# Sparse attention with soft mixture of experts on one core: the first transfers in a fixed order, larger load pieces, another table of priorities

## The chip, the core and the metric

The kernel runs on one NeuronCore of a Trainium2 chip. All data are fp32. The core has a matrix engine (TensorE, PE in the profile), VectorE (DVE), ScalarE (ACT), GpSimd (POOL) and SyncE (SP), which only issues transfers here. Each takes its instructions from its own list in the order in which they were written; semaphores hold an instruction back until what it needs is there. Transfers run on 16 DMA engines that all issuers share. The metric is the time of one execution on the device in microseconds (us), as the median of several runs.

## What is computed

Block-sparse attention feeds a soft mixture of experts. Cut to what matters:

```python
# q, k, v: [4, 8, 768, 64]; 24 blocks of 32 rows; 3 sampled blocks per block row
scores = (q @ k.T) / 8
mask   = |bi - bj| <= 1, or bi or bj is the first or the last block, or bj in sampled_blocks[bi]
attn   = softmax(where(mask, scores, -1e9)) @ v          # -> x [3072, 512]

logits = x @ phi                                          # [3072, 32]: 8 experts x 4 slots
d = softmax over the 3072 rows;  slots = d.T @ x          # [32, 512]
slot_out[e] = relu(slots[e] @ w1[e]) @ w2[e]              # FF = 1024
out = softmax over the 32 slots of logits @ slot_out      # [3072, 512]
```

## The kernel before

**Attention.** The four batches follow one another. The first and the last block row of a batch see all 24 blocks ("dense", two tasks per batch); the other 22 are taken in eleven pairs ("pair"). These tasks are numbered n = 0, 1, 2 ... over all batches; batch 0 begins with a dense task (n = 0), then the first pair (n = 1). For a pair, POOL and ACT copy the key blocks that it sees into a staging buffer `kst` (window and global blocks on POOL at L538 and L540, the three sampled blocks on ACT at L546 or on POOL at L548), and POOL copies the sampled value blocks into `vrs` (L564). Its queries are loaded (`q`, L407, 128 KB) and scaled in place by POOL (L583) or ACT (L581). PE makes scores `s` (L619), DVE their negative maximum `nm` (L636), ACT the exponentials `p` (L641), DVE transposes them in blocks of 32 into `ptt` (L648), and PE multiplies them with the values `v` and `vrs` (`av`, L713). DVE divides and writes the tile `x` (L706 to L708). The dense tasks do the same with `sd`, `nb`, `pd`, `ptd`, `avd` (L815, L841, L846, L850), directly from `ktile` and `v`. Score tiles `s`, `sd` and the warm-up's `st` take turns in four PSUM buffers.

**Grouping.** Four finished tiles `x` make a group: PE transposes them (`mxt`, L906), makes logits (`ml`), and adds up the dispatched rows with a running maximum (`md`, `ms`).

**Experts.** Afterwards 64 weight pieces of 512 KB are multiplied in turn: `w1` (`pf`, L1331), then `w2` (`pso`, L1339); the combine (`po`, L1435) follows in two column halves, and SP stores the result, 6.29 MB.

**Places of the weights.** 11 pieces have room from the beginning. 15 more are loaded into the room of attention's `ktile`, `v0`, `ptd` and again `ktile` (there they are called `kw`) towards the end of attention; these are the early weights. The late weights are issued after the planned part: ten into free room (`w26` to `w31`, `w36` to `w39`), six into the room of `v1`, and two into the last two `ptt` buffers (`w42`, `w43`); each further piece follows when an earlier one has been used. All are issued on SP.

**What sets the order.** In attention and grouping each step is a task of a plan (`Plan.add`): a function, the engines that may run it with a cost, the tasks that it depends on, a key, the buffers that it takes (`acq`) and the bytes of its transfer. A list scheduler goes through these tasks: of those that can start soonest it takes the one with the smallest key plus `BEHIND[kind]`, where the kind is the function that made the task. So a table of 79 numbers sets the order of PE, DVE, ACT, POOL and SP, and the choice of engine where there are several. `after` is a dependence on another task's start alone. What is written outside the plan ahead of it (in the kernel before: `ident`, an identity matrix built by POOL, and `sel4`, built from it by DVE and ACT) stands where it is written. Behind the plan PE, DVE, ACT and POOL keep the order of the code, and SP's is set by the framework's scheduler.

**The start.** POOL fills `ident` (masks.py:197 and 199). DVE and POOL clear the halves of `v0`, ACT those of `v1` (L465, by scaling a column of `ident` with 0). ACT loads the sampled block numbers (`scr`, L357) and the `q` of n = 1. SP loads the first `q`, K of batch 0 in four pieces (L420), `phi` (L1118), V of batch 0 in eight pieces (L431), and further `q`. PE runs 12 matmuls on `ident` to warm up (L479).

**Pieces.** `LR = 32` is the number of rows in one K load of the batches 1 to 3 and in one load of an early weight; `VC` the number of value blocks in one V load (13 for batch 0, 7 for the others); `LCOLS` cuts the last `kw` and the first ten late weights into two loads of 512 columns.

Of the kernel before, what the change touches and what calls it, by code (L numbers as in the profile page):

```python
# [15 lines left out]
ALU = mybir.AluOpType  # L16
# [27 lines left out]
LR, RATE = 32, 0.22  # L44

LC = 512
# [13 lines left out]
LCOLS = [slice(c, c + LC) for c in range(0, WP, LC)]  # L60
# [6 lines left out]
BEHIND = {0: -83.25, 1: -13.2, 2: -52.5, 3: 75.2, 4: 62.8, 5: 11, 6: -77.2, 7: -48.45, 8: -12.95, 9: -4.65, 10: 6.3,  # L67
# [30 lines left out]
FETCH, PACKET = 3.5, 256  # L98
# [10 lines left out]
class Plan:  # L109
# [29 lines left out]
    def plan(self, turn, best=1e9):  # L139
# [14 lines left out]
        while avail:  # L154
# [50 lines left out]
            elif e == "SP":  # L205
                dma = max(dma, st + 2.2) + self.byte[t] / 0.39e6
                fin = dma + 0.3
            elif e == "NONE":
                fin = st
            else:  # L210
                fin = en + LAG[e]
# [69 lines left out]
def attn_moe_kernel(ctx, tc, qT, kT, vtab, sampled, phi, w1, w2, out):  # L281
# [49 lines left out]
    def w_of(n, c):  # L331
# [5 lines left out]
    make_identity(nc, ident)  # L337
    sel4 = const.tile([P, P], F32, name="sel4")
    DVE.tensor_reduce(out=sel4[:, 0:NS], in_=ident.rearrange("p (c s) -> p s c", c=4),
                      axis=AX.X, op=ALU.add)  # L340
    for c in range(1, 4):
        ACT.copy(out=sel4[:, c * NS:(c + 1) * NS], in_=sel4[:, 0:NS])
# [68 lines left out]
    VC = lambda b: 7 if b else 13  # L411
# [48 lines left out]
    t_idx = add(lambda t: index_load(), ("ACT", 2.0), [], -40)  # L460

    def clear(b, a):
        half = vbuf[b][:, a * VH:(a + 1) * VH]
        if b:
# [3 lines left out]
    t_zero = [[add(clear(b, a), (("DVE", "POOL")[a], 2.7) if b == 0 else ("ACT", 2.85), [], -45 if b == 0 else -35 + a)  # L468
               for a in range(2)] for b in range(2)]

# [1057 lines left out]
```

## Time and profile before

| | |
|---|---|
| median of 3 runs | 310.47 us (310.13, 311.16, 310.47) |
| profiled execution | 312.11 us, of which span 310.3 us from the first instruction to the last |
| mean granted PE clock | 0.969 |
| instructions | 17664 |
| ACT, POOL busy | 175.4 us (57%), 179.6 us (58%) |
| DMA | 60.30 MB, mean 194 GB/s; HBM read 52.86 MB, written 6.29 MB |
| instruction loads (queue q8) | 57 packets, 0.93 MB |

All durations below come from the one profiled execution. Its time outside the span is 312.11 − 310.3 = 1.8 us. A row of the timeline has start, duration, engine, line, operation, tile written and tiles read, count, and in brackets the idle time of the engine ahead of it and what ended that. "ACTq" and "SPq" are the instruction queues of ACT and SP; their rows are the issues of transfers. A releaser is inferred from semaphores: with several, it is the last by the profile.

### The profile page before, as it was taken

How to read it: one execution, taken by the hardware profiler on the slowest of the kernel's cores; microseconds unless marked ns; L12 is line 12 of the kernel's file. 1: busy time of each engine (PE TensorE's matmuls, PEld its weight loads, DVE VectorE, ACT ScalarE, POOL GpSimd, SP SyncE). 2: the span in 40 equal slices, each digit the busy share in tenths (PEclk: the TensorE clock that was granted, in tenths of full speed). 3: DMA queues.
4: the chain of work that ended last, by engine and by line, in shares of the span. 5: the costliest groups of instructions: out<-in, count | busy, mean ns of one | idle time of the engine just before them, and what ended most of it. 6: DMA issues, size and time to landing. Idle time of an engine off the chain costs nothing.

```text
span 310.3 us, 17664 instructions
## 1 busy us (share of the span) xinstructions
PE 277.2 (89%) x7181; PEld 198.6 (64%) x7181; DVE 217.1 (70%) x500; ACT 175.4 (57%) x525; POOL 179.6 (58%) x491
## 2 busy tenths in 40 slices
PE   4388998999999799999999999999997899999950
PEld 4137876676777567768676777877676673355540
DVE  7477996768989487998998878998876225012350
ACT  6657786763677586647877863697630141102440
POOL 5589479964946968784589967569766014000000
PEclk9979999999999979999999999999997999999996
DMA  7924556320256743024465420677689999999998
GB/s 239 228 60 124 167 168 181 111 88 3 60 171 183 209 118 109 5 89 139 137 201 158 127 72 23 204 214 220 191 222 311 380 359 413 406 410 406 323 270 273
DMA packets 31971, 60.30 MB, mean 194 GB/s; under 512 B 5265, under 2 KB 18706, under 8 KB 31890
## 3 DMA queue, kind: packets, MB, share of 16 engines
q1 hardware_dynamic: 31744, 59.04, 59.7%
q8 instruction: 57, 0.93, 1.3%
q14 instruction: 24, 0.20, 0.2%
q10 hardware_dynamic: 146, 0.13, 0.2%
HBM read 52.86 MB, written 6.29 MB: 191 GB/s over the span
## 4 chain that ended last, share of the span: by engine, by line
PE 75%; DVE 9%; issue 4%; ACT 2%; DMA 2%; POOL 2%; POOLq 1%; SPq 1%; ACTq 0%; DVEq 0%
PE av L713 32%; PE s L619 11%; PE avd L713 5%; PE pso L1339 5%; PE pf L1331 5%; PE mxt L906 4%; PE sd L815 3%; DMA ktile<-in_kT_dram 2%; PE ms L991 2%; DVE ptd L850 2%; PE st L479 2%; PE po L1435 2%; PE ml L941 2%; DVE x L708 2%; DVE nm L636 1%
## 5 line engine op out<-in xcount | busy, mean ns | idle before, releaser
L564 POOL COPY vrs<-v 128x260 f32 x264 | 95.8, 405 | 30.8 <-PE av L713 23.0
L641 ACT ACTIVATE p<-s,nm 128x256 f32<-128x256 f32 x176 | 73.5, 475 | 15.8 <-DVE nm L636 12.1
L713 PE MATMUL av<-v,ptt 64*64 64x130 f32 (+2 forms) x1728 | 76.8, 290 | 1.2 <-PE md L982 0.8
L713 PEld LDWEIGHTS av<-v,ptt 64*64 64x64 f32 (+2 forms) x1728 | 51.2, 134 | 26.8 <-issue 19.4
L636 DVE TENSOR_REDUCE nm<-s 128x2 f32<-128x512 f32 x88 | 55.1, 680 | 5.6 <-PE s L619 5.2
L619 PE MATMUL s<-kst,q 64*32 64x256 f32 x1408 | 50.3, 386 | 8.3 <-POOL q L583 4.9
L648 DVE STREAM_TRANSPOSE ptt<-p 128x512 f32<-128x512 f32 x88 | 56.2, 682 | 1.7 <-ACT p L641 1.5
L540 POOL COPY kst<-ktile 128x384 f32<-128x384 f32 x88 | 42.9, 507 | 14.2 <-PE s L619 13.2
L713 PE MATMUL av<-vrs,ptt 64*32 64x130 f32 x2112 | 46.5, 278 | 3.5 <-issue 3.5
L546 ACT ACTIVATE kst<-ktile 128x128 f32 x186 | 41.5, 302 | 11.6 <-PE s L619 8.5
L619 PEld LDWEIGHTS s<-kst,q 64*32 64x32 f32 x1408 | 31.2, 107 | 17.3 <-POOL q L583 5.6
L713 PEld LDWEIGHTS av<-vrs,ptt 64*32 64x32 f32 x2112 | 35.9, 106 | 5.4 <-issue 5.3
L448 ACT COPY xT<-mxt 128x512 f32<-128x512 f32 (+1 forms) x22 | 12.5, 566 | 27.0 <-PE mxt L906 25.9
L713 PE MATMUL avd<-v,ptd 64*64 64x130 f32 x768 | 23.2, 271 | 1.3 <-DVE ptd L850 1.2
L713 PEld LDWEIGHTS avd<-v,ptd 64*64 64x64 f32 x768 | 21.8, 132 | 3.3 <-PE s L619 2.2
L548 POOL COPY kst<-ktile 128x128 f32 x78 | 19.9, 293 | 0.2 <-issue 0.2
L846 ACT ACTIVATE pd<-sd,nb 128x384 f32<-128x384 f32 x32 | 16.9, 579 | 4.3 <-DVE nb L841 4.1
L581 ACT ACTIVATE q<-q 128x256 f32<-128x256 f32 x27 | 11.2, 417 | 13.2 <-DMA q<-in_qT_dram 13.1
L815 PE MATMUL sd<-ktile,q 64*32 64x384 f32 x256 | 17.1, 504 | 1.3 <-ACT p L641 1.3
L706 DVE TENSOR_SCALAR rs<-av 128x8 f32<-128x8 f32 (+1 forms) x27 | 4.2, 157 | 19.7 <-PE av L713 19.5
L906 PEld LDWEIGHTS mxt<-ident,x 128*128 128x128 f32 x96 | 10.9, 147 | 11.2 <-DVE nm L636 2.5
L906 PE MATMUL mxt<-ident,x 128*128 128x128 f32 x96 | 16.9, 298 | 1.2 <-DVE x L695 0.9
(122 smaller groups left out, 305.2 us busy)
## 6 DMA issues: line engine op xcount, KB each, us to landing
w<-in_w_dram SPq DMA_DIRECT2D x17, 512.0 KB, 9.7
q<-in_qT_dram SPq DMA_DIRECT2D x47, 128.0 KB, 2.5
w<-in_w_dram SPq DMA_DIRECT2D x44, 128.0 KB, 3.3
out_dram<-ob SPq DMA_DIRECT2D x22, 256.0 KB, 3.2
ktile<-in_kT_dram SPq DMA_DIRECT2D x48, 96.0 KB, 2.7
v<-in_w_dram SPq DMA_DIRECT2D x8, 512.0 KB, 10.2
v<-in_vtab_dram SPq DMA_DIRECT2D x36, 113.8 KB, 3.2
v<-in_w_dram SPq DMA_DIRECT2D x24, 128.0 KB, 3.6
```

The lines of the kernel that those rows point to most:

```text
L540: POOL.tensor_copy(out=st[:, :, w:w + 96], in_=kv[:, :, (i - 1) * BLK:(i + 2) * BLK])
L546: ACT.activation(out=st[:, :, o:o + BLK], in_=src, func=AF.Copy, scale=1.0)
L548: POOL.tensor_copy(out=st[:, :, o:o + BLK], in_=src)
L564: POOL.tensor_copy(out=st[:, :, j:j + 1, :], in_=vf[:, :, ds(t.vals[j], 1), :])
L619: PE.matmul(u.s[r][32 * p:32 * p + 32, j, :], lhsT=u.q[s_, p, j, :], rhs=kd[j][0][s_, p, :], start=True, stop=True)
L636: DVE.tensor_reduce(out=u.nm[r], in_=u.s[r], axis=AX.X, op=ALU.max, negate=True)
L641: ACT.activation(out=u.p[r][:, j, :], in_=u.s[r][:, j, :], func=AF.Exp, bias=u.nm[r][:, j:j + 1], scale=1.0)
L648: DVE.transpose(out=T.pt[r][:, :, 2 * w:2 * w + 2, :].rearrange("p k j q -> p j k q"), in_=u.p[r].rearrange("p j (k q) -> p j k q", k=8))
L713: PE.matmul(av[:, r * 2 * D1:(r + 1) * 2 * D1].rearrange("p (a d) -> p a d", a=2), lhsT=lhsT, rhs=rhs, start=start, stop=stop)
L815: PE.matmul(u.s[r][k][32 * p:32 * p + 32, :], lhsT=T.dq.q[s_, p, j, :], rhs=kt[s_, p, 384 * k:384 * (k + 1)], start=True, stop=True)
L846: ACT.activation(out=u.p[r][k], in_=u.s[r][k], func=AF.Exp, bias=u.nb[r], scale=1.0)
L906: PE.transpose(T.px[:, c, :], T.x[:, c * P:(c + 1) * P], ident)
```

## The change

Five things are changed.

1. `make_identity` and the making of `sel4` become tasks of the plan (`t_ident`, `sel_head`, `sel_rest`); what reads `ident` or `sel4` depends on them.
2. The first transfers are chained by `after` in a fixed order (`seq`): the first `q`, K, the `q` of n = 3 and n = 4, V in an interleaved order, `phi`. ACT issues the `q` of n = 1 right behind the index load, and clears `v1` only behind that.
3. `LR` becomes 64 and `VC` 13 for all batches: K, V and the early weights are loaded in pieces about twice as large.
4. `LCOLS` goes: the last `kw` and the first ten late weights are loaded whole.
5. `BEHIND` gets other numbers (82 kinds now), and four of the planner's costs change: `FETCH`, SP's bytes per us, and ACT's cost of an issue.

SP's first rows, before (with the number of the tile behind each name):

```order
L407 DMA q0_97<-in_qT_dram 128x256
L420 DMA ktile_112<-in_kT_dram 128x2x384 x4
L1118 DMA phis_80<-in_phi_dram 128x128
L431 DMA v0_68<-in_vtab_dram 32x1690 x4
L431 DMA v0_68<-in_vtab_dram 32x1560 x4
L407 DMA q2_99<-in_qT_dram 128x256
```

and after (`q0_...`, `q1_...`, `q2_...` and `q3_...` are the four buffers for queries, used here by n = 0, 1, 3 and 4; `v0` is V of batch 0):

```order
L400 DMA q0_89<-in_qT_dram 128x256
L413 DMA ktile_110<-in_kT_dram 128x2x384 x4
L400 DMA q2_91<-in_qT_dram 128x256
L400 DMA q3_92<-in_qT_dram 128x256
L424 DMA v0_68<-in_vtab_dram 32x1690
L424 DMA v0_68<-in_vtab_dram 32x1560
L424 DMA v0_68<-in_vtab_dram 32x1690
```

`phi` went behind V, and two `q` came ahead of it; the pieces of V alternate in size.

ACT's first rows, before (`ISA` ahead of a copy sets its block number):

```order
L357 DMA scr_86<-in_sampled_dram 1x144
L465 ACT_TABLE_LOAD
L465 ACTIVATE v1_69<-ident_70 128x3250
L342 COPY sel4_75<-sel4_75 128x32 x3
L465 ACTIVATE v1_69<-ident_70 128x3250
L407 DMA q1_98<-in_qT_dram 128x256
L436 TENSOR_LOAD sreg_84
L846 ACTIVATE pd_226<-sd_158,nb1_209 128x384
```

and after:

```order
L350 DMA scr_78<-in_sampled_dram 1x144
L400 DMA q1_90<-in_qT_dram 128x256
L466 ACT_TABLE_LOAD
L466 ACTIVATE v1_69<-ident_70 128x3250 x2
L429 TENSOR_LOAD sreg_76 x2
L461 COPY sel4_71<-sel4_71 128x32 x3
L549 ISA
L549 ACTIVATE kst0_85<-ktile_110 128x4x32
...
L549 ACTIVATE kst1_86<-ktile_110 128x4x32
...
L584 ACTIVATE q3_92<-q3_92 128x256
L851 ACTIVATE pd_231<-sd_157,nb1_215 128x384
```

The `q` of n = 1 (`q1_...`) moved from behind the first clear and the copies of `sel4` to the second row. Six copies of sampled key blocks (L549, three each into `kst0` and `kst1`) and one scaling of a `q` now stand ahead of the first `pd` exponentials, where there were none.

SP's rows where the late weights begin, before:

```order
L308 DMA kw_6654<-in_w1_dram 128x512 x4
L308 DMA w26_7125<-in_w1_dram 128x512 x2
L308 DMA w27_7128<-in_w1_dram 128x512 x2
L308 DMA w28_7131<-in_w1_dram 128x512 x2
L308 DMA w29_7134<-in_w1_dram 128x512 x2
L308 DMA w30_7137<-in_w1_dram 128x512 x2
L308 DMA w31_7140<-in_w1_dram 128x512 x2
L308 DMA v1_69<-in_w2_dram 128x512 x8
L308 DMA w36_7151<-in_w2_dram 128x1024
```

and after:

```order
L306 DMA kw_6562<-in_w1_dram 128x1024 x3
L306 DMA v1_69<-in_w2_dram 128x1024 x4
L306 DMA w42_7052<-in_w2_dram 128x1024
L306 DMA v1_69<-in_w2_dram 128x1024
L306 DMA w26_7026<-in_w1_dram 128x1024
L306 DMA w27_7028<-in_w1_dram 128x1024
L306 DMA w28_7030<-in_w1_dram 128x1024
L306 DMA w29_7032<-in_w1_dram 128x1024
L306 DMA w30_7034<-in_w1_dram 128x1024
```

Six weights `w26` to `w31`, which stood ahead of `v1`, went behind five pieces of `v1` and `w42`; `w42` takes the room of a `ptt` buffer of the last tile. On PE the rows are the same in the same order, but for one group of warm-up matmuls ahead of the last tile's transposes, which has 6 instead of 8. On ACT and POOL the copies into `kst` and `vrs` and the scalings of `q` change places throughout.

The diff, with the old and new table cut to a line each:

```diff
@@ -41,9 +41,7 @@
 
 LD0, LD1 = 3, 12
 
-LR, RATE = 32, 0.22
-
-LC = 512
+LR, RATE = 64, 0.22
 
 CS = 2
 CW = DM // CS
@@ -57,21 +55,21 @@
 
 
 LORD = [0, 1, 2, 3, 4, 5, -1, -2, -3, -4, 6, 7, 8, 9, -5, -6, 10, 11]
-LCOLS = [slice(c, c + LC) for c in range(0, WP, LC)]
 H1, HALF = 3, 4
 CPES = [0, 0, 3, 3, 3, 2, 0, 0]
 HEAD = -4096
 E_ = mybir.EngineType
 MAN = {E_.PE, E_.DVE, E_.Activation, E_.Pool}
 
-BEHIND = {0: -83.25, 1: -13.2, 2: -52.5, 3: 75.2, 4: 62.8, 5: 11, 6: -77.2, 7: -48.45, 8: -12.95, 9: -4.65, 10: 6.3,
...
+BEHIND = {0: -44.85, 1: -125.35, 2: -87.1, 3: -125.75, 4: 74.55, 5: 85.55, 6: 172.75, 7: -50.15, 8: -162.05, 9:
...
 SOON = 0.03
 LAG = {"DVE": 0.17, "ACT": 0.18, "POOL": 0.17, "SP": 0.0, "NONE": 0.0}
 SP_COST = 0.55
@@ -95,7 +93,7 @@
     "slots": (0.3, 0.65, "R", "R", 8),
 }
 TURN = {"T": 0.17, "N": 0.32, "M": 0.3, "R": 0.3, "C": 0.2}
-FETCH, PACKET = 3.5, 256
+FETCH, PACKET = 3.7, 256
 
 
 class Task:
@@ -203,7 +201,7 @@
                 count += n
                 fin = st + rel
             elif e == "SP":
-                dma = max(dma, st + 2.2) + self.byte[t] / 0.39e6
+                dma = max(dma, st + 2.2) + self.byte[t] / 0.36e6
                 fin = dma + 0.3
             elif e == "NONE":
                 fin = st
@@ -334,12 +332,7 @@
 
 
     ident = const.tile([P, P], F32, name="ident")
-    make_identity(nc, ident)
     sel4 = const.tile([P, P], F32, name="sel4")
-    DVE.tensor_reduce(out=sel4[:, 0:NS], in_=ident.rearrange("p (c s) -> p s c", c=4),
-                      axis=AX.X, op=ALU.add)
-    for c in range(1, 4):
-        ACT.copy(out=sel4[:, c * NS:(c + 1) * NS], in_=sel4[:, 0:NS])
     phis = const.tile([P, 4, NS], F32, name="phis")
     lst = const.tile([P, B * NT, NS], F32, name="lst")
     sacc = const.tile([P, DM], F32, name="sacc")
@@ -408,7 +401,7 @@
         return q
 
 
-    VC = lambda b: 7 if b else 13
+    VC = lambda b: 13
 
     def new_k(b):
         ktile[b] = pk.tile([P, NP, S], F32, name="ktile", tag="ktile")
@@ -457,7 +450,15 @@
         pass
 
 
-    t_idx = add(lambda t: index_load(), ("ACT", 2.0), [], -40)
+    t_idx = add(lambda t: index_load(), ("ACT", 0.6), [], -60)
+    t_ident = add(lambda t: make_identity(nc, ident), ("POOL", 0.6), [], -60)
+
+    def sel_head(t):
+        DVE.tensor_reduce(out=sel4[:, 0:NS], in_=ident.rearrange("p (c s) -> p s c", c=4), axis=AX.X, op=ALU.add)
+
+    def sel_rest(t):
+        for c in range(1, 4):
+            ACT.copy(out=sel4[:, c * NS:(c + 1) * NS], in_=sel4[:, 0:NS])
 
     def clear(b, a):
         half = vbuf[b][:, a * VH:(a + 1) * VH]
@@ -465,8 +466,9 @@
             return lambda t: ACT.activation(out=half, in_=ident[:, 0:1].to_broadcast([P, VH]), func=AF.Copy, scale=0.0)
         return lambda t: (DVE, POOL)[a].memset(half, 0.0)
 
-    t_zero = [[add(clear(b, a), (("DVE", "POOL")[a], 2.7) if b == 0 else ("ACT", 2.85), [], -45 if b == 0 else -35 + a)
+    t_zero = [[add(clear(b, a), (("DVE", "POOL")[a], 2.7) if b == 0 else ("ACT", 2.85), [t_ident], -45 if b == 0 else -35 + a)
                for a in range(2)] for b in range(2)]
+    t_zero[0][0].deps.clear()
 
     def sreg_copy(t):
         sraw = scr[0:1, 0:NB * NR * 2].bitcast(I32).rearrange("p (i j w) -> p i j w", i=NB, j=NR)
@@ -479,7 +481,7 @@
             PE.matmul(st[:, 0, 0:P], lhsT=ident, rhs=ident, start=True, stop=True)
 
     use = []
-    t_warm = add(warm, ("PE", "warm"), [], -41, acq=[("s", use)])
+    t_warm = add(warm, ("PE", "warm"), [t_ident], -41, acq=[("s", use)])
     use.append(t_warm)
     t_sreg = add(sreg_copy, ("DVE", 0.3), [t_idx], -39)
     t_vreg = add(lambda t: index_math(), ("DVE", 4.0), [t_sreg], -38)
@@ -492,7 +494,7 @@
     first = {b: min(n for n, i in enumerate(items) if i[0] == b) for b in range(B)}
 
     k_use, v_use = ([[] for _ in range(B)] for _ in range(2))
-    t_k, t_v, t_first = {}, {}, []
+    t_k, t_v, t_first, boot = {}, {}, [], {}
     qks = {}
 
     def plan_loads(b):
@@ -513,9 +515,10 @@
                               pace=b > 0))
             else:
                 vs.append(add(lambda t, c=c: load_v(b, *c[1:]), ("SP", SP_COST), go + [a_v] + (t_zero[b] if b < 2 else []), key,
-                              byte=114000 if b else 208000, pace=b > 0))
+                              byte=208000, pace=b > 0))
         if not b:
             t_first.extend(ks[:2])
+            boot["k"], boot["v"] = ks, vs[0::4] + vs[2::4] + vs[1::4] + vs[3::4]
         t_k[b] = add(lambda t: None, ("NONE", 0.0), ks, -30)
         t_v[b] = add(lambda t: None, ("NONE", 0.0), vs, -30)
         k_use[b].append(t_k[b])
@@ -582,7 +585,9 @@
             else:
                 POOL.tensor_scalar(out=u.q, in0=u.q, scalar1=SCALE, scalar2=1.0, op0=ALU.mult, op1=ALU.mult)
 
-        t_q = add(load, ("ACT", 2.0) if n == 1 else ("SP", SP_COST), [], n - 6 if n > 4 else -19.65 if n > 2 else -30, acq=[("q", use)], byte=131072)
+        t_q = add(load, ("ACT", 0.6) if n == 1 else ("SP", SP_COST), [], n - 6 if n > 4 else -19.65 if n > 2 else -30, acq=[("q", use)], byte=131072)
+        if n < 5:
+            boot[n] = t_q
         t_q = add(scale, [("POOL", 0.37), ("ACT", 0.37)], [t_q], n - 4.5)
         use.append(t_q)
         return t_q, use
@@ -1116,6 +1121,7 @@
     t_end = None
     plan_loads(0)
     t_phi = add(lambda t: SP.dma_start(out=phis, in_=phi), ("SP", 0.4), [], -18.5, byte=65536)
+    t_sel = add(sel_rest, ("ACT", 0.9), [add(sel_head, ("DVE", 0.4), [t_ident], 20)], 21)
     N = len(items)
     for n, (b, c) in enumerate(items):
         if isinstance(c, str):
@@ -1125,6 +1131,12 @@
         for b1 in range(1, B):
             if n == first[b1] - 1:
                 plan_loads(b1)
+    seq = [boot[0], *boot["k"], boot[3], boot[4], *boot["v"], t_phi]
+    for a, b in zip(seq, seq[1:]):
+        b.after.append(a)
+    boot[1].after.append(t_idx)
+    for t in t_zero[1]:
+        t.after.append(boot[1])
     done.sort(key=lambda z: z[0])
     for gi in range(6):
         Ts = done[4 * gi:4 * gi + 4]
@@ -1144,7 +1156,7 @@
         for j in range(KW[tag]):
             parts = [(slice(r, r + LR), slice(0, WP)) for r in range(0, P, LR)]
             if n0 == 12:
-                parts = [(slice(0, P), c) for c in LCOLS]
+                parts = [(slice(0, P), slice(0, WP))]
             for i, (r, c) in enumerate(parts):
                 add(lambda t, m=m, tag=tag, j=j, r=r, c=c: load_wk(m, tag, j, r, c), ("SP", SP_COST), go(j) + [a_w],
                     N + m + j + i / 4, byte=4 * WP * P // len(parts), pace=n0 < 12)
@@ -1213,7 +1225,7 @@
     t_2 = add(f_exp, ("ACT", 0.25), [t_1], k)
     t_3 = add(f_col, ("PE", "col"), [t_2], k, acq=[("pt", u[1])])
     row_use.append(t_3)
-    t_4 = add(f_sel, ("ACT", 0.55), [t_3], k, acq=[("lp", lp_use)])
+    t_4 = add(f_sel, ("ACT", 0.55), [t_3, t_sel], k, acq=[("lp", lp_use)])
     u[1].append(t_4)
     t_end = add(lambda t: f_slots(t, 0), ("PE", "slots"), [t_4, state.t_acc0], k + 1, acq=[("pt", u[2])])
     t_end = add(lambda t: f_slots(t, 1), ("PE", "slots"), [t_end, state.t_acc], k + 1)
@@ -1283,11 +1295,10 @@
     def load_late(pool, j=None):
 
         m = len(wpool)
-        for c in LCOLS if m < MLATE else [slice(0, WP)]:
-            if j is None:
-                load_w(m, pool, None, slice(0, P), c)
-            else:
-                load_wk(m - j, pool.tag, j, slice(0, P), c)
+        if j is None:
+            load_w(m, pool)
+        else:
+            load_wk(m - j, pool.tag, j)
         wpool.append(pool)
 
     for tag in EARLYW:
@@ -1308,7 +1319,6 @@
     load_group(LATEW[0], False)
 
     new_wk(LATEW[1])
-    MLATE = len(wpool) + 10
     lw, vw = [Place(lwb, f"w{n}") for n in range(NLB)], Group(LATEW[1])
     lw += [Place(pw, f"ptt{(nt[0] + r) % PTB}") for r in (2, 3)]
     for n in LORD:
```

15 rows, old and new, of the table BEHIND are left out of this document.

## The prediction

> **What bounds the kernel now.** I read the page first, the engines' totals and the chain of waits, and then PE's waits one by one.
>
> ```profile
> PE 277.2 (89%) x7181; PEld 198.6 (64%) x7181; DVE 217.1 (70%) x500; ACT 175.4 (57%) x525; POOL 179.6 (58%) x491
> PE 75%; DVE 9%; issue 4%; ACT 2%; DMA 2%; POOL 2%; POOLq 1%; SPq 1%; ACTq 0%; DVEq 0%
> PE s L619 <- POOL q L583: 4.9, 1, 4.9
> PE st L479 <- POOL ident masks.py:199: 4.1, 1, 4.1
> PE s L619 <- POOL vrs L564: 1.9, 1, 1.9
> ```
>
> TensorE (PE) is busy for 89% of the span and makes 75% of the chain, so time can be won only where PE stands idle or runs at a lower clock. The last three rows are PE's own waits (total, times, longest). The two largest are single events at the start. The wait for `ident` costs nothing by itself, because the warm-up matmuls that it holds back feed nobody; the wait for `q` does. Next I read the timeline of the start.
>
> ```profile
> 0.87 2.81 POOL L466 MEMSET v<- 128x3250 f32 x1
> 3.72 0.29 POOL masks.py:199 TENSOR_SCALAR_AFFINE_SELECT ident<-ident 128x128 f32<-128x128 f32 x1
> 4.04 2.91 ACT L465 ACTIVATE v<-ident 128x3250 f32<-128x3250 f32 x1 [1.46 <-POOL ident masks.py:199]
> 7.25 0.36 ACTq L407 DMA_DIRECT2D q<-in_qT_dram  x1
> 9.10 0.40 POOL L538 COPY kst<-ktile 128x256 f32<-128x256 f32 x1 [4.30 <-DMA ktile<-in_kT_dram]
> 11.10 0.16 DVE L841 TENSOR_TENSOR nb<-nm 128x1 f32<-128x1 f32 x1
> 11.36 1.05 ACT L846 ACTIVATE pd<-sd,nb 128x384 f32<-128x384 f32 x2 [1.25 <-DVE nb L841]
> 12.30 0.70 ACT L546 ACTIVATE kst<-ktile 128x128 f32 x3
> 12.90 1.05 ACT L846 ACTIVATE pd<-sd,nb 128x384 f32<-128x384 f32 x2
> 14.57 0.40 POOL L583 TENSOR_SCALAR q<-q 128x256 f32<-128x256 f32 x1 [2.21 <-DMA q<-in_qT_dram]
> 15.03 1.96 PE L619 MATMUL s<-kst,q 64*32 64x256 f32 x32 [4.89 <-POOL q L583]
> 17.90 2.14 POOL L564 COPY vrs<-v 128x260 f32 x6
> 21.08 1.24 PE L713 MATMUL av<-v,ptt 64*64 64x130 f32 x20
> 27.35 0.44 PE L713 MATMUL avd<-v,ptd 64*64 64x130 f32 x4 [0.80 <-DVE ptd L850]
> ```
>
> The chain backwards from the first score matmul: `s` at 15.03 waits for POOL's scaling of tile 1's `q` (14.57), that for a transfer which ACT issued only at 7.25, because ACT was held by the first clear of `v` (4.04), that by `ident` (3.72), and `ident` by POOL's own 2.81 us clear (0.87). So a small mask built late holds up a load, and through it PE for 4.89 us. After 28 us PE hardly stops until the expert weights' stage.
>
> **Part 1, the start.** The new order builds `ident` ahead of POOL's clear and issues q1 directly behind the index load, before ACT's clears. q1 can then be issued at about 0.74 + 0.53 = 1.3 us (end of the index load's issue) instead of 7.25. Even with the same 14.57 − 7.25 = 7.3 us to landing it is there at 8.6, before anything can use it. What is late next? By the order, `s` waits for the first `pd` exponentials, which free its PSUM buffers, and for the `kst` copies. In front of these `pd` exponentials ACT now has six copies of `kst` (2 × 0.70) and one scaling of q (0.42, half of a row below). K lands a little later, since q1's 128 KB share the way: at the 355 GB/s of the slice from 4 to 8 us that is 0.4 us.
>
> ```profile
> 4.00:8.00 4.00, 3.94 (x20) 3.94 (x21) 3.52 (x18) 3.96 (x5) 0.80 (x3) 1.00 1.10 355
> 11.00:15.00 4.00, 0.00 (x0) 0.00 (x0) 1.91 (x6) 2.59 (x7) 1.79 (x7) 0.93 1.01 230
> 15.00:16.00 1.00, 0.97 (x24) 0.57 (x32) 0.00 (x0) 0.00 (x0) 0.77 (x2) 0.50 1.02 196
> 105.77 0.42 ACT L581 ACTIVATE q<-q 128x256 f32<-128x256 f32 x1 [1.12 <-DMA q<-in_qT_dram]
> ```
>
> (The columns of a slice are its length, busy time of PE, PEld, DVE, ACT and POOL with counts, granted clock, DMA share, GB/s.) K's copies can start at 9.1 + 0.4 = 9.5; ACT's share of 1.4 and 0.42 ends at 11.4; `nb` is ready at 11.10 + 0.4 = 11.5; the two exponentials take 1.05: `s` at about **12.6 instead of 15.03, −2.4 us**. Bounds: if neither K's delay nor ACT's copies counted and one exponential were enough, 11.36 + 0.53 = 11.9 (−3.1); if all four had to be done, as far behind the first two as now (12.90 − 11.36), 12.6 + 1.5 = 14.1 (−0.9).
>
> Is the gain carried to `av`? Before, `av` came 21.08 − 15.03 = 6.05 us behind `s`; so 18.65 now. V must be there: its copies into `vrs` began at 17.90. Two q loads of 128 KB are put ahead of V and phi's 64 KB behind it: 192 KB, at 230 GB/s 0.85 us, so V is there at about 18.7. The two come together; I take −2.4 for `av`, too. `avd` then waits for less: its transposes stand earlier on DVE, but I count nothing for that.
>
> One thing could add to it. PE ran the first `s` at clock 0.50 behind its idle 4.89 us (slice 15 to 16: 32 matmuls took 1.96 us). After an idle time of 2.3 us the clock may still be 1.00, and then up to 0.98 us less is spent there. [...] I count zero, because V's landing hides it, and keep −0.98 for the range.
>
> **Part 2, new priorities for ACT, POOL and SP.** By the order PE's sequence is the same, so only waits can come or go. Two stalls in the middle show the price of one.
>
> ```profile
> 107.97 1.30 ACT L546 ACTIVATE kst<-ktile 128x128 f32 x6
> 108.77 1.30 PE L619 MATMUL s<-kst,q 64*32 64x256 f32 x32 [1.86 <-POOL vrs L564]
> 108.00:112.00 4.00, 3.23 (x43) 2.09 (x45) 3.10 (x9) 3.15 (x13) 4.00 (x13) 0.75 0.42 131
> 112.00:116.00 4.00, 4.00 (x100) 2.41 (x98) 3.53 (x7) 3.63 (x13) 1.64 (x5) 0.82 0.39 111
> 235.25 0.63 PE L713 MATMUL av<-vrs,ptt 64*32 64x130 f32 x19 [1.73 <-issue]
> 236.00:240.00 4.00, 4.00 (x22) 3.76 (x23) 2.70 (x11) 0.03 (x1) 3.00 (x8) 0.57 1.00 345
> ```
>
> At 108.77 the trace names POOL, but what ended last is the first three of ACT's `kst` copies at 107.97, which stood behind a scaling of q that waited 1.12 us for its transfer (105.77). Idle 1.86, and then a lower clock: 4 × 0.25 + 4 × 0.18 = 1.7 us. One such stall costs **3.6 us**. It may go, stay, or come elsewhere (0 to −3.6 here, +3.6 for a new one). ACT's and POOL's rows are reshuffled throughout, and PE's other waits in the middle are below 1 us; I take 0, nearest to the many places where covers of 2 to 4 us hold.
>
> **Part 3, K and weight pieces of 64 rows, V of 13 blocks.** Fewer issues on SP, same bytes.
>
> ```profile
> 104.00:108.00 4.00, 2.91 (x116) 2.09 (x112) 0.27 (x1) 2.47 (x8) 3.23 (x10) 1.00 0.70 199
> 240.00:244.00 4.00, 3.60 (x104) 2.78 (x108) 0.00 (x0) 0.56 (x1) 0.00 (x0) 1.00 1.06 387
> 257.00:300.00 43.00, 41.34 (x464) 21.79 (x464) 13.97 (x40) 11.41 (x26) 3.57 (x6) 1.00 1.00 376
> ```
>
> At 199 GB/s, 128 KB more in front of a q load delay it by 0.65 us; that is the price where a q stands behind one piece and nothing covers it. The share of 0.70 leaves room; cover is the time by which q is issued ahead, so 0, with +0.65 as the end for each uncovered place. [...]
>
> **Part 4, late weights whole.** Halves already moved at 387 GB/s (240 to 244) and wholes at 376 (257 to 300): nothing to gain in rate. The order matters more: of the twelve halves issued from 232.77, six wholes now stand behind `w42`, which waits for the last tile's `ptt` to be read, while four wholes of `v1` stand ahead.
>
> ```profile
> 232.77 9.53 SPq L308 DMA_DIRECT2D w<-in_w_dram  x12
> 242.73 5.22 SPq L308 DMA_DIRECT2D v<-in_w_dram  x8
> 270.27 2.76 PE L1331 MATMUL pf<-w,sT 128*32 128x512 f32 x24
> 278.62 1.59 SPq L308 DMA_DIRECT2D w<-in_w_dram  x2
> 292.12 1.05 PE L1339 MATMUL pso<-w,hT 128*32 128x256 f32 x16
> w<-in_w_dram SPq DMA_DIRECT2D x17, 512.0 KB, 9.7
> ```
>
> The six moved weights are used at 270.27 at the earliest, over 20 us after the move. What counts is the whole stream: its last load is issued at about 279.9, lands 9.7 later at 289.6, and is used at 292.12: a cover of 2.5 us. If the stream keeps its old time while PE comes 2.4 us earlier, the cover is just used up, at no cost. Moved ahead are 4 × 512 KB, moved behind 6; by 376 GB/s the stream could lag by 2 × 1.4 = 2.8 us, or, since the start of `v1` moves to POOL's last read of it, gain as much. I take 0 and keep ±2.8.
>
> **Sum.** Against the profiled execution (span 310.3, 312.1 in all): −2.4 + 0 + 0 + 0 = 309.7. The median before is 310.47, so **308.1**.
>
> **Rivals.**
> - *A stall goes as well*: the one at 108.8 disappears, since its copies are dealt out anew, and perhaps the first `s` at full clock. For it: ACT's share there was late by one q load. 308.1 − 3.6 = 304.5. Chance 0.22.
> - *Slower: a new stall of the kind at 108.8.* A q load behind a doubled piece lands 0.65 us later, and ACT or POOL, which wait for it in order, hold `kst` copies that PE needs. ACT waited for q 13.1 us in 12 places, POOL 12.6 in 9, so places abound. One stall at 3.6 already decides: 308.1 + 3.6 = 311.7. Against it: most are covered. Chance 0.20.
>
> ```profile
> ACT q L581 <- DMA q<-in_qT_dram: 13.1, 12, 3.3
> POOL q L583 <- DMA q<-in_qT_dram: 12.6, 9, 3.3
> ```
>
> - *The gain is given back*: V or `vrs` holds the first `av` at its old time, or the weight stream lags by 2.8 us behind an unmoved end of the loads, so that PE waits at the last experts: 310.5. It decides when V lands 2.4 us late or the stream 2.5. Chance 0.10.
> - *The change does not do what it says*: q1 is early, but the clears or the six `kst` copies on ACT hold the exponentials until 14: −0.9, 309.6. Chance 0.05.
>
> **How the numbers follow.** The forecast itself, 306.5 to 309.4, has 0.43. Range: 304.0 (stall gone and 0.5 of the clock) to 312.2 (a new stall, and one uncovered 0.65). The ends leave out two stalls more or fewer. A difference below 0.3%, 0.9 us, cannot be told from none: below 309.5 lie the forecast and the first rival, 0.65; within, the gain given back and the late exponentials, 0.15; above 311.4, the new stall, 0.20.
>
> **What would show it.** After: the first `s` near 12.6 without a wait for q; `av` near 18.7 and `avd` near 25; PE's rows between 30 and 230 earlier by the same 2.4 us; the last late weight landing before its matmul; no PE wait above 1.5 us in the middle. I am wrong if the first `s` comes after 14, if `av` waits for V, or if the shift at 28 us is not found again at 257.

## The result and the profile after

The changed kernel takes **319.64 us** (median of 4 runs, 318.51 to 321.52); the kernel before took 310.82 beside it (4 runs). The ratio is 1.0298 (95% interval 1.0232 to 1.0363): slower by 3%, where 308.1 was forecast and 304.0 to 312.2 given as range. The profiled execution has a span of 319.7 us (310.3 before). Ratios, here and below, leave out runs that are over 1.5% above the fastest of the same kernel; medians do not.

The page of the changed kernel, with the engines' totals, the instruction queue and the chain:

```profile
PE 281.7 (88%) x7177; PEld 199.7 (62%) x7177; DVE 217.5 (68%) x500; ACT 171.9 (54%) x519; POOL 182.0 (57%) x497
q8 instruction: 56, 0.92, 1.3%
PE 74%; DVE 8%; issue 7%; DMA 5%; ACT 2%; SPq 1%; ACTq 0%; DVEq 0%
```

"issue", time in which an engine waits for nothing that the profile shows, went from 4% of the chain to 7%. PE's waits of the changed kernel (total, times, longest) say where (four of its rows):

```profile
PE av L718 <- issue: 15.1, 13, 2.5
PE s L624 <- issue: 2.6, 3, 1.7
PE s L624 <- ACT pd L851: 1.9, 1, 1.9
PE ml L946 <- issue: 0.5, 1, 0.5
```

The wait for `q` at the start (4.9 us) is gone. Instead there are 18.2 us of "issue", where the kernel before had 3.9 + 1.6 = 5.5. The start itself came out better than forecast; the timeline of the changed kernel:

```profile
1.29 0.36 ACTq L400 DMA_DIRECT2D q<-in_qT_dram  x1
6.46 1.79 PE L820 MATMUL sd<-ktile,q 64*32 64x384 f32 x24
8.57 0.40 POOL L541 COPY kst<-ktile 128x256 f32<-128x256 f32 x1 [2.93 <-DMA ktile<-in_kT_dram]
9.95 0.27 DVE L846 TENSOR_TENSOR nb<-nm 128x1 f32<-128x1 f32 x1
10.45 1.03 ACT L851 ACTIVATE pd<-sd,nb 128x384 f32<-128x384 f32 x2
11.15 1.47 PE L624 MATMUL s<-kst,q 64*32 64x256 f32 x32 [1.85 <-ACT pd L851]
17.70 2.26 PE L718 MATMUL av<-v,ptt 64*64 64x130 f32 x36
23.29 0.44 PE L718 MATMUL avd<-v,ptd 64*64 64x130 f32 x4 [0.75 <-DVE ptd L855]
```

`s` is at 11.15 instead of 15.03 and `avd` at 23.29 instead of 27.35: 4.06 us won. Where they were lost again shows when the start of the same matmuls is set side by side, from the two timelines (us; the last column is from the profile of run e1 below):

| first matmul of | before | changed | changed against before | e1 against before |
|---|---|---|---|---|
| `avd` | 27.35 | 23.29 | −4.06 | −4.95 |
| `mxt` of the 1st tile | 35.57 | 32.19 | −3.38 | −4.94 |
| `mxt` of the 5th tile | 69.33 | 71.05 | +1.72 | −5.07 |
| `mxt` of the 8th tile | 99.45 | 101.34 | +1.89 | −6.44 |
| `mxt` of the 12th tile | 134.23 | 133.30 | −0.93 | −5.21 |
| `mxt` of the 19th tile | 202.65 | 204.68 | +2.03 | −4.17 |
| `mxt` of the 20th tile | 211.15 | 216.82 | +5.67 | −4.52 |
| `pf`, the first expert | 257.17 | 266.99 | +9.82 | −5.02 |
| `po`, the last | 299.81 | 309.63 | +9.82 | −5.01 |

From −4.06 to +9.82, 13.9 us are lost. Two stretches cost 12.9 of them: 32 to 71, when K and V of the second batch and four weight pieces are loaded, and 204 to 267, the time of the early and the first late weights. From the first expert on nothing more is lost. Between 71 and 204 a gain and a loss hide each other. From the 8th to the 12th tile the changed kernel wins 2.8 us: the stall of 1.86 us that the kernel before has at 108.77 is gone, and PE's longest wait there is 0.50. From the 12th to the 19th it loses 3.0. One of the stalls, in the changed kernel:

```profile
208.73 1.71 PE L718 MATMUL av<-v,ptt 64*128 64x130 f32 x40
209.30 5.20 SPq L306 DMA_DIRECT2D v<-in_w_dram  x3
210.23 0.68 PE L718 MATMUL av<-vrs,ptt 64*32 64x130 f32 x31
213.39 0.52 PE L718 MATMUL av<-vrs,ptt 64*32 64x130 f32 x17 [2.48 <-issue]
```

and the same place in the kernel before:

```profile
208.00 0.42 PE L713 MATMUL av<-vrs,ptt 64*32 64x130 f32 x15
208.74 0.74 PE L713 MATMUL av<-vrs,ptt 64*32 64x130 f32 x33 [0.31 <-issue]
```

PE stops in the middle of 48 like matmuls whose data are there. What is missing is the program: the queue of instructions (q8) brought 56 packets of 0.92 MB / 56 = 16 KB. PE's 7177 matmuls and 7177 weight loads make 14354 / 56 = 256 for each packet, so the packets are PE's. Counted over the recorded matmuls and weight loads, all long stalls stand at a place modulo 256 that drifts slowly, from 172 to 56, and PE goes on a nearly fixed time behind the landing of a packet:

```
changed kernel: instruction, modulo 256 | packet on the DMA engines | PE goes on | after landing
 1964   172   45.15 to  46.52    47.94   1.42
 2472   168   54.97 to  55.95    57.45   1.50
 2982   166   65.24 to  66.55    67.95   1.40
 8549   101  162.01 to 163.07   164.63   1.57
11334    70  210.58 to 211.87   213.39   1.52
12601    57  237.04 to 238.06   239.38   1.32
13112    56  249.16 to 250.13   251.47   1.34
```

(What makes the place drift slowly was not shown; the count has the recorded matmuls and weight loads alone.) The before kernel's stall at 235.25 is of the same kind: packet landed at 234.01, PE on 1.24 later. With every boundary interpolated from these places, a packet began in the median about 1.5 us after PE had crossed the boundary before it in the changed kernel, and about 1.2 in the kernel before (estimates, as the places are interpolated).

After such a stop the clock was low, too, as in the changed kernel behind the stall at 67.95 (0.64):

```profile
68.00:72.00 4.00, 4.00 (x54) 2.42 (x56) 2.89 (x7) 0.26 (x1) 2.75 (x8) 0.64 0.02 4
```

### The profile page after: what moved, and what is told of

It is laid out like the page before. It is cut to its first block, busy times and chain, and to the rows that moved or that the text cites. A ratio compares the mean times of both kernels' runs of the same rounds, so it can differ in the third digit from the quotient of the medians.

```text
span 319.7 us, 17465 instructions
## 1 busy us (share of the span) xinstructions
PE 281.7 (88%) x7177; PEld 199.7 (62%) x7177; DVE 217.5 (68%) x500; ACT 171.9 (54%) x519; POOL 182.0 (57%) x497
## 4 chain that ended last, share of the span: by engine, by line
PE 74%; DVE 8%; issue 7%; DMA 5%; ACT 2%; SPq 1%; ACTq 0%; DVEq 0%
PE av L718 32%; PE s L624 12%; PE avd L718 7%; PE pf L1341 4%; PE mxt L911 4%; PE pso L1349 3%; DMA out_dram<-ob 3%; PE ml L946 2%; PE sd L820 2%; PE ms L996 2%; DMA ktile<-in_kT_dram 2%; DVE x L713 1%; DVE ptd L855 1%; PE st L481 1%; DVE nm L838 1%
## 5 line engine op out<-in xcount | busy, mean ns | idle before, releaser
L646 ACT ACTIVATE p<-s,nm 128x256 f32<-128x256 f32 x176 | 72.8, 475 | 23.7 <-DVE nm L641 21.5
L718 PEld LDWEIGHTS av<-v,ptt 64*64 64x64 f32 (+2 forms) x1728 | 50.5, 133 | 28.7 <-issue 21.6
L718 PE MATMUL av<-vrs,ptt 64*32 64x130 f32 x2112 | 49.3, 278 | 12.6 <-issue 12.4
L624 PE MATMUL s<-kst,q 64*32 64x256 f32 x1408 | 51.0, 386 | 4.5 <-issue 2.6
L549 ACT ACTIVATE kst<-ktile 128x128 f32 x186 | 41.2, 302 | 12.2 <-PE s L624 10.9
L624 PEld LDWEIGHTS s<-kst,q 64*32 64x32 f32 x1408 | 33.8, 107 | 11.3 <-issue 4.7
L820 PE MATMUL sd<-ktile,q 64*32 64x384 f32 x256 | 17.9, 574 | 1.2 <-ACT p L646 1.0
L713 DVE TENSOR_TENSOR x<-av,rs 128x512 f32<-128x512 f32 (+1 forms) x27 | 16.5, 611 | 0.9
## 6 DMA issues: line engine op xcount, KB each, us to landing
v<-in_w_dram SPq DMA_DIRECT2D x12, 512.0 KB, 10.2
```

The costliest lines, as they stand in the source:

```text
L549: ACT.activation(out=st[:, :, o:o + BLK], in_=src, func=AF.Copy, scale=1.0)
L624: PE.matmul(u.s[r][32 * p:32 * p + 32, j, :], lhsT=u.q[s_, p, j, :], rhs=kd[j][0][s_, p, :], start=True, stop=True)
L646: ACT.activation(out=u.p[r][:, j, :], in_=u.s[r][:, j, :], func=AF.Exp, bias=u.nm[r][:, j:j + 1], scale=1.0)
L713: DVE.tensor_tensor(out=x, in0=a[:, :, :, 0:D], in1=rs[lo:hi].unsqueeze(3).to_broadcast([hi - lo, 2, 2 * n, D]), op=ALU.mult)
L718: PE.matmul(av[:, r * 2 * D1:(r + 1) * 2 * D1].rearrange("p (a d) -> p a d", a=2), lhsT=lhsT, rhs=rhs, start=start, stop=stop)
L820: PE.matmul(u.s[r][k][32 * p:32 * p + 32, :], lhsT=T.dq.q[s_, p, j, :], rhs=kt[s_, p, 384 * k:384 * (k + 1)], start=True, stop=True)
```

## Experiments

The theories: **A**, transfers twice as large hold PE's instruction packets up; **B**, the new priorities make the stalls; **C**, the whole late weights do; **D**, the earlier start does, by moving packets against loads. PE's order is the same in all whole kernels, but for the fill-in group told of with the change. Ratios are to the kernel before in the same session, with their 95% interval. The kernel before had medians of 311.4 to 312.1 in these sessions, with single runs from 307.7 to 316.8.

### Which part

**e9, the pieces alone**, in the kernel before:

```diff
-LR, RATE = 32, 0.22
+LR, RATE = 64, 0.22
-    VC = lambda b: 7 if b else 13
+    VC = lambda b: 13
-                              byte=114000 if b else 208000, pace=b > 0))
+                              byte=208000, pace=b > 0))
```

> The kernel before with pieces of 64 rows and 13 blocks alone; start, table and late halves stay as before. If large transfers by themselves make the stalls: 318 to 326, PE's issue waits above 14 us (5.5 before). If they do so only together with the earlier start or the new table: 309 to 313.

327.23 us (324.78 to 331.18), ratio 1.0586 (1.0477 to 1.0695). PE's waits:

```profile
PE av L713 <- issue: 16.6, 16, 2.2
PE s L619 <- issue: 2.2, 4, 0.8
```

The pieces by themselves cost 16 us, more than the whole change and just above the range expected. Not all of it is the stalls: in its profile the first expert comes 8.5 us later than in the kernel before (265.68), the last `po` 13.7 (313.48). The other 5.2 us are lost among the experts, where the clock was 0.93 instead of 1.00 and PE waits for late weights:

```profile
PE pso L1339 <- DMA w<-in_w_dram: 1.3, 2, 0.7
PE pso L1339 <- DMA v<-in_w_dram: 1.3, 3, 0.6
```

**e4, the start alone**, in the kernel before: points 1 and 2 of the change, with the old table (its numbers given to the same functions).

> The kernel before with the new start alone (identity first, first transfers in the fixed order); old table, pieces and halves. Theories A, A2, B and C: only the start's gain is left, 306 to 308. Theory D (an earlier start shifts PE's instruction packets against the loads and so makes the stalls): 313 to 319. If the start's gain is lost behind V: 309.5 to 311.

310.65 us (10 runs, 306.74 to 314.40), ratio 0.9929 (0.9864 to 0.9995). PE's waits for issue stay near those before (6.6 us with one of 0.6 at `md`, after 5.5):

```profile
PE av L712 <- issue: 4.2, 6, 1.7
PE s L618 <- issue: 1.8, 2, 1.1
```

No new stalls, so D falls. The ratio is worth 2.2 us (0.71% of 311); in its profile `s` came at 12.96 and the first expert 2.45 us earlier than before. The median alone would fit the last of the three expectations, but the gain was not lost behind V: it reached the experts.

**e3, everything but the table:**

```diff
-BEHIND = {0: -44.85, 1: -125.35, ...
+BEHIND = {0: -83.25, 1: -125.35, 2: -13.2, ...
-FETCH, PACKET = 3.7, 256
+FETCH, PACKET = 3.5, 256
-                dma = max(dma, st + 2.2) + self.byte[t] / 0.36e6
+                dma = max(dma, st + 2.2) + self.byte[t] / 0.39e6
```

> The changed kernel with the old table of priorities and the old costs of transfers and fetches; start, pieces of 64 rows and whole late weights stay. Theories A and A2: stalls stay, 315 to 320. Theory B: PE's issue waits fall to 4 to 6 us and the time to 306 to 309.

325.51 us (322.49 to 327.39), ratio 1.0388 (1.0272 to 1.0504), issue waits 18.9 + 3.5 us. B falls: with the old table the stalls are there as well, and the median is higher still than the changed kernel's, and above the 315 to 320 that A gave.

**e2, everything but the pieces** (the edit of e9 the other way, in the changed kernel):

> The changed kernel with pieces of 32 rows and of 7 blocks as before, each planned and paced by itself; the start, the table and the whole late weights stay. Theories A and A2 (pieces): issue waits of PE below 9 us, time 308 to 313. Theory B (priorities): 317 to 321. Theory C (the late weights loaded whole): 317 to 321, with PE's stalls of 1.6 to 1.8 us at 239 and 251 unchanged.

309.57 us (304.62 to 312.07) beside 311.73. Issue waits fall to 7.0 us. The late weights are whole here, so C is no large part; one stall of 3.7 us, at 232, stays.

### What about the pieces

**e1, halves with the same plan.** In the changed kernel each piece is issued as two transfers, one behind the other; the plan and the orders of PE, DVE, ACT and POOL are those of the changed kernel row by row, and SP's differs by the halves and in the order of the late loads.

```diff
-        return SP.dma_start(out=ktile[b][rows, p, :], in_=kT[b, p, rows])
+        rows = [slice(r, r + 32) for r in range(rows.start, rows.stop, 32)]
+        return [SP.dma_start(out=ktile[b][r, p, :], in_=kT[b, p, r]) for r in rows][0]
...
-        i = SP.dma_start(out=vb[s_, a % 2, lo:hi], in_=vtab[b, s_, lo:hi])
+        m = lo + 7 * 2 * D1
+        cuts = [(lo, m), (m, hi)] if b else [(lo, hi)]
+        i = [SP.dma_start(out=vb[s_, a % 2, l:h], in_=vtab[b, s_, l:h]) for l, h in cuts][0]
```

(and early weights in rows, as K).

> The changed kernel with its plan untouched; only each 64-row piece of K and of an early weight is issued as two transfers of 32 rows back to back, each 13-block piece of V of batches 1 to 3 as 7 and 6 blocks. Theory A (a single large transfer holds the DMA engines, so that PE's 16 KB instruction packet starts late): PE's waits put down to issue fall from 17.7 us to below 9, and the time to 310 to 313. Theory A2 (what counts are the bytes that are bunched in front of the packet, not the size of one transfer): the same bytes are issued at the same places, so 317 to 321. Theory B (the new priorities make the stalls): 317 to 321, too.

**306.0 us** (305.10 to 308.87), ratio 0.9845 (0.9741 to 0.9949): 13.6 us below the changed kernel's 319.64, faster than both kernels, and below even the 310 to 313 of theory A. PE's waits:

```profile
PE av L723 <- issue: 3.9, 3, 1.8
PE s L629 <- issue: 0.7, 2, 0.4
PE avd L723 <- issue: 0.4, 1, 0.4
```

The last column of the table above is its profile: it keeps 5.0 us to the end. The same bytes were issued at the same points of the plan, so it is not their bunching (A2) but how a transfer is cut. Cutting also puts one issue of SP between the halves (SP's four K issues at the start took 1.95 us, so about 0.5 each); size and this spacing are not told apart.

**e5, only V in halves** (V's part of the edit above):

> The changed kernel, same plan; only the V pieces of batches 1 to 3 are issued as 7 and 6 blocks, K and weights stay at 64 rows. If the long rows of V (6760 B) hold up the instruction packets: 306 to 311. If the 64 rows of K and weights do: 316 to 320, PE's issue waits above 12 us.

316.52 us (10 runs, 310.84 to 322.83), ratio 1.0069 (1.0002 to 1.0136); its profile, of a run of 317.8, still has 18.5 us of issue waits. Median and waits are those of the second expectation; the ratio, below the changed kernel's 1.0298, says that V's halves help, too.

**e6, only K and the early weights in halves by rows**, and **e7, in halves by columns** (64 rows as before, two transfers of half the columns each):

```diff
-        return SP.dma_start(out=ktile[b][rows, p, :], in_=kT[b, p, rows])
+        return [SP.dma_start(out=ktile[b][rows, p, c], in_=kT[b, p, rows, c]) for c in (slice(0, S // 2), slice(S // 2, S))][0]
...
```

(and the early weights alike).

> The changed kernel, same plan; only K and the early weights are issued as two transfers of 32 rows, V stays at 13 blocks. If the 64-row transfers are the cause: 306 to 310, issue waits below 8 us; if V is: 316 to 320.

> The changed kernel, same plan; K and early weights are issued as two transfers of 64 rows and half the columns, so as many bytes in each as in the 32-row halves, V stays. If the bytes of one transfer count: as in the run with row halves of K and weights alone, within 2 us. If the 64 rows as such count: 316 to 320.

By rows 311.09 us (309.38 to 315.31), ratio 1.0016 (0.9964 to 1.0068). So both kinds of piece count: by the ratios, halves of V alone take back 2.3 points of the change, halves of K and the weights 2.8, and both together (e1) 4.5. By columns 317.54 (317.22 to 318.73), ratio 1.0233 (1.0127 to 1.0339). PE's waits for issue with rows,

```profile
PE av L721 <- issue: 7.1, 9, 2.3
PE s L627 <- issue: 1.9, 2, 1.1
```

and with columns:

```profile
PE av L720 <- issue: 7.8, 9, 1.7
PE s L626 <- issue: 0.9, 2, 0.7
```

With 9.4 us in all, rows just miss their first expectation (below 8, and 306 to 310 in time). Rows and columns are alike (9.4 and 8.9), so the time alone would mislead: column halves relieve the packets in this profile as well. They lose it elsewhere. ACT's waits for `q`, with columns:

```profile
ACT q L586 <- DMA q<-in_qT_dram: 28.3, 11, 5.3
```

With rows it is 12.8 us. With columns q lands late, and PE waits for the copies behind it (4.9 us for POOL's `vrs`, 0.3 with rows). Neither of the two expectations of e7 holds alone.

### The late weights

**e8**, e1 with the last three `kw` and `w26` to `w31` in four transfers of 32 rows; **e10**, only the `kw`:

```diff
+QUART = (23, 24, 25, 26, 27, 28, 29, 30, 31)
...
+        cut = [slice(r, r + 32) for r in range(rows.start, rows.stop, 32)]
+        if rows.stop - rows.start == P and m not in QUART:
+            cut = [rows]
```

> The run with halves (306.0), and also the last three kw and w26 to w31 issued as four transfers of 32 rows each instead of one of 512 KB. Theory A: the two last long issue stalls (1.79 us at 230.9 and 238.6) go, 302.5 to 305, unless the stream of late weights, slower to issue, makes PE wait at the last experts: then 306 to 309. If those stalls have nothing to do with the size of transfers: 305 to 307 with both still there.

> The run with halves (306.0), and only the last three kw in four transfers of 32 rows each; w26 to w31 whole. The stall at 230.9 (1.79 us) goes, that at 238.6 may stay, and the stream lags by less than its cover: 303 to 305.5 with no PE wait for weights. If even this lag is too much: 306 to 309 with such waits at L1357.

e8: 309.04 us (10 runs, 306.03 to 312.12), ratio 0.9928 (0.9873 to 0.9983). The two long stalls of e1 (1.79 us each, at 230.90 and 238.59) went, but PE waits for weights, as the second half of the expectation has it:

```profile
PE pso L1357 <- DMA w<-in_w_dram: 1.9, 3, 0.6
PE av L726 <- issue: 1.8, 4, 0.7
PE pso L1357 <- DMA v<-in_w_dram: 1.5, 3, 0.6
PE pso L1357 <- DMA kw<-in_w_dram: 1.1, 2, 0.6
```

The stretch from 224 to 248 in e8,

```profile
224.00:248.00 24.00, 21.38 (x453) 16.40 (x450) 13.19 (x45) 7.32 (x22) 8.40 (x21) 1.00 0.88 225
```

moved 225 GB/s; in e1 it was 351. The first expert began 7.9 us earlier than in the kernel before, the last `po` only 1.45. e10: 309.00 (306.02 to 316.57), ratio 0.9934 (0.9883 to 0.9985); a stall of 1.25 stays at 230 and one of 2.34 at 238, and PE waits for no weight, so neither of its expectations holds. Neither run beats e1.

These three runs also show how far one profile can be trusted. e1, e8 and e10 issue the same transfers in the same order until 225 us, and up to 210 us their profiles have 1.4, 1.6 and 3.8 us of issue waits. The changed kernel (10.2), e3 (12.3) and e9 (12.0) lie far outside this scatter.

### The packets measured by themselves

**e11** computes nothing of the reference: PE runs tiny matmuls without a break, SP loads in stretches of one shape at one pace (DVE clears the place of each transfer first).

> Not the kernel: nothing of the reference is computed and the output is zeros. PE runs 7920 tiny matmuls with nothing to wait for, while SP loads at one pace, first nothing, then in turn 32x1024, 64x1024, two 64x512, two 32x1024, 128x1024, two 128x512 and V rows of 910 and 1690 columns. If the height of a transfer delays PE's packets: the time between two packets is longer in the phases with 64 and 128 rows than in those with 32, and the same for 64x1024 and 64x512; by the whole kernel some 0.5 us. If only bytes in flight count: 64x1024 and two 32x1024 alike.

Here PE uses a packet of 256 in about 4.0 us (931 + 929 matmuls and weight loads in the 29.30 us of the first row below), so only late ones show. The stretches are 32x1024, 64x1024, two 64x512, two 32x1024, 128x1024, two 128x512, and V rows of 910 and 1690 columns (columns: length, busy time of PE, PEld, DVE, POOL, clock, DMA share, GB/s):

```profile
14.60:43.90 29.30, 29.30 (x931) 29.30 (x929) 25.38 (x44) 0.00 (x0) 1.00 0.61 183
52.80:84.20 31.40, 31.18 (x971) 30.85 (x969) 25.19 (x44) 0.00 (x0) 1.00 0.52 171
92.50:126.40 33.90, 33.14 (x1032) 32.81 (x1030) 26.97 (x48) 0.00 (x0) 1.00 0.51 159
132.20:163.40 31.20, 31.20 (x991) 31.20 (x989) 24.93 (x44) 0.00 (x0) 1.00 0.55 173
173.50:204.90 31.40, 30.03 (x939) 29.78 (x937) 24.23 (x43) 0.00 (x0) 1.00 0.54 171
214.40:245.70 31.30, 31.16 (x981) 31.00 (x978) 24.23 (x43) 0.00 (x0) 1.00 0.61 171
252.90:281.90 29.00, 29.00 (x922) 29.00 (x920) 25.35 (x48) 0.00 (x0) 1.00 0.65 185
290.80:319.50 28.70, 28.70 (x911) 28.70 (x909) 24.00 (x28) 0.00 (x0) 1.00 0.65 185
```

PE is busy for the whole stretch with 32 rows, in singles, pairs and V, and loses 0.14 to 1.37 us with 64 or 128, at a rate that is no higher (159 to 171 GB/s against 173 to 185).

**e12**, the same with matmuls fast enough for PE to be bound by its packets (64x32 by 16 columns, on eight parts of the array in turn; without loads it is busy for 10.69 of 28.00 us):

> Not the kernel, output nearly zeros: PE runs 9920 tiny matmuls (64x32 by 16 columns, in turn on eight parts of the array), fast enough that it waits for its instructions, while SP loads at one pace: first nothing, then 32x1024, 64x1024 (rows 0 to 63 and 64 to 127 in turn), 64x1024 (always rows 32 to 95), two 64x512, two 32x1024, 128x1024, two 16x1024. The time for one packet of 256 instructions is read for each stretch. [...] Estimate from the kernels: 0.5 us more for 64 rows than for 32.

```
mean time from one packet to the next, us (packets in the stretch)
no loads                     3.62  (75)
two 16x1024, 100 GB/s        3.73  (14)
two 32x1024                  3.95   (8)
32x1024                      4.12   (7)
128x1024                     4.22   (6, longest 5.26)
two 64x512                   4.25   (8)
64x1024, rows 32 to 95       4.39   (7)
64x1024, rows 0-63, 64-127   4.55   (7, longest 5.24)
```

So loads lengthen the way of a packet by 0.3 to 0.5 us in pieces of 32x1024 and by 0.8 to 0.9 in pieces of 64x1024. Rows 32 to 95 (4.39) are hardly better than 0 to 63 and 64 to 127 in turn (4.55), and 128 rows (4.22) are not the longest. With six to eight packets in a stretch a mean is uncertain by 0.1 to 0.2 us, that of 128 rows by 0.3, so only the main difference is clear: taken together, the two stretches with 32 rows have 4.03 ± 0.10 us, the three with 64 rows 4.37 ± 0.09 (mean and standard error), 0.34 apart where 0.5 was estimated.

## Why the prediction was wrong

- **Part 3 failed.** It put the larger pieces at 0; alone they cost 16 us (e9, 327.2). "The share of 0.70 leaves room; cover is the time by which q is issued ahead, so 0" looked for one passenger behind the pieces, the q loads, and valued it well (ACT waited for q 13.1 us before and 10.7 after). The other was left out: PE's program, which the profile lists among the queues of the same 16 DMA engines (1.3%) and which, as far as the traces show, is fetched only one packet ahead: a packet began after PE had crossed the boundary before, by the interpolated places some 1.5 us after in the changed kernel and 1.2 in the kernel before. In the kernel before, PE's packets began 4.2 us apart (median, 29 to 230 us). Where PE waits for nothing else, one packet followed another in 3.6 us without other loads, 4.0 to 4.1 beside 32 rows of 1024 and 4.4 to 4.6 beside 64 (e12). So with 32 rows PE's program just kept up, and with 64 it did not. Shown by e9, by e1 (the same plan with halves, 306.0), and by the two probes.
- **The signs were there.** One is the row `PE av L713 <- issue: 3.9, 6, 1.7` of the kernel before, with the stall at 235.25, which the prediction shows without asking what PE waits for there. "The engine waited for nothing that the profile shows" is a question, not an answer. The other is in the diff: the planner's `FETCH, PACKET = 3.5, 256`, which the change raises to 3.7. In `Plan.plan` these hold PE to at least `FETCH` us for every `PACKET` instructions, so the kernel's own cost model had the term that the prediction left out.
- **The rival for slower** had the right place (behind doubled pieces) and the wrong passenger. Its price for a stall, 3.6 us with the clock, was too high: there were seventeen of 1.1 us in the mean (18.2 in all, after nine with 5.5). Between the first `avd` and the first `pf` PE was idle for 21.5 us instead of 10.4, and busy for 222.2 instead of 219.5 for the same matmuls, at a granted clock of 0.97 instead of 0.99: of the 13.9 us lost, 11.1 are idle time and 2.7 the clock.
- **The rival for a stall that goes** saw its event: the one at 108.77 went, worth 2.8 us instead of 3.6. Its reason is not shown. e1 has the same orders on PE, DVE, ACT and POOL, and there PE waits 2.05 us at 102.96 for ACT's `kst` copies again; the changed kernel comes to the 8th tile 8.3 us later than e1, so the copies may simply have had the time.
- **Part 1 was right in kind and too small**: −2.4 forecast for `s`, −3.9 measured, beyond the bound of −3.1. `sd` came at 6.46 instead of 8.62, as the warm-up that it stands behind began at 1.36 instead of 4.07: the wait for `ident`, which I had called free, was worth something. `nb` came at 9.95, not 11.5, and K was not later (8.57 against 9.10). V did not hold `av`, which came at 17.70, right behind PE's `sd`.
- **Part 2's 0 for the table** holds within the scatter with small pieces: e2 (start, table, whole late weights) has a median of 309.57, e4 (start alone) 310.65. With large pieces it is not settled: the medians are 325.51 and 319.64, from two sessions, and the intervals of their ratios overlap (1.0272 to 1.0504 and 1.0232 to 1.0363).
- **Part 4's 0 for the end of the stream** holds: the first expert and the last `po` are both 9.82 us later, and PE waits for no weight. Not seen was that loads of 512 KB in this place stall the packets, too: with quarters in their place (e8) the two stalls of 1.79 us were gone, and the slower stream (225 GB/s from 224 to 248 instead of 351) gave more back.
- **The clock**: the mean was 0.958 after 0.969. The first `s`, behind 1.85 us of idle time instead of 4.89, took 1.47 us for 32 matmuls (granted clock 0.97 from 11 to 13 us) instead of 1.96 (0.50 from 15 to 16), so part of the reserve of 0.98 us was there.
- **Its own sign of being wrong** came: the shift of −4.06 at `avd` was not found again at the first expert (+9.82).

What in the engines makes a packet wait is not settled. Beside the loads of e12 a packet took longer than the 3.62 us without loads by 0.50 with 32x1024, 0.93 with 64x1024, 0.77 with rows 32 to 95, 0.63 with two 64x512 and 0.60 with 128x1024, so not in the order of the rows of a load. In the kernel single waits are longer: at the stall at 67.95 PE had crossed the boundary at about 61.7 (interpolated), and the packet began at 65.24. Whether halves of a transfer are worth it for the load itself no run here tests, as the probes load at a set pace; in e1 the halves of the 64-row pieces win 13.6 us through another queue, that of the instructions.

Open also are why column halves bring q late, and how far e1 is from e2 (306.0 and 309.57, ranges that overlap).

## What to carry to other kernels

Where PE runs through its instructions as fast as here, one packet of 256 in about 4 us (4.2 in the kernel before), its program is a load like any other: look for "issue" waits at equal distances in the instruction count before changing the size of transfers. Cut bulk loads that run beside such a stretch into smaller transfers (here 32 rows instead of 64: 306.0 us in e1 instead of 319.64), even if the plan hands them out in large ones. Where the stream of loads itself has no time to spare, leave them large: in e8 the quarters cost more than the stalls that they took away (309.04 us, and 306.0 in e1). A part of the change that only "makes fewer transfers" should be run alone first: here it cost 16 us alone and hid a gain of 5.

## What the runs showed that I had not expected

- The way of a packet went with the shape of the loads beside it, and not with their rate alone: in e12 3.95 to 4.12 us with 32 rows of 1024 at 181 and 191 GB/s, 4.39 to 4.55 with 64 at 175 and 180.
- PE went on 1.3 to 1.6 us after its packet had landed in the seven stalls of the table above, and 1.24 in that of the kernel before at 235.25.
- A V row of 6760 B took 427 ns on its engine in the changed kernel, one of 3640 B 197 in the kernel before (means of the batches 1 to 3): 15.8 and 18.5 B per ns, so the long rows were no faster.
